# First loads in another order over the two DMA queues, with the work that follows them on VectorE, ScalarE and TensorE reordered

## The chip, the cores and the metric

The kernel runs on one core of a Trainium2 chip. A core has five engines, each with its own in-order instruction stream: TensorE (PE in the profile, its weight loads PEld), VectorE (DVE), ScalarE (ACT), GpSimd (POOL) and SyncE (SP). SP and ACT issue the transfers of this kernel; 16 DMA engines carry them out. The metric is the time of one execution on the device in microseconds (us).

## The reference

One transformer block with adaptive layer norm: 2048 tokens of width 512, 32 heads of 16, a feed-forward width of 1792, all in bf16. The part that matters here is the first layer norm with its modulation, and the projections that read its result.

```python
mod = (_silu(c) @ w_mod).reshape(c.shape[0], 6, 1, -1)
sa, ca, ga, sb, cb, gb = (mod[:, 0].copy(), ...)
h = _layernorm(x, axis=-1) * (1 + ca) + sa
x = x + ga * _A_ref(h, A_wqkv, A_wo)          # attention, softmax over 2048 keys
h = _layernorm(x, axis=-1) * (1 + cb) + sb
x = x + gb * _B_ref(h, B_w_gate, B_w_up, B_w_down)
```

`sa` is the first block of 512 columns of `silu(c) @ w_mod`, `ca` the second.

## The kernel before

The kernel has a prologue and a stream. The prologue (`prologue`, from L499) loads what the first 512 tokens need and brings them as far as q and k of the first heads; the stream then runs the attention of 32 heads, the output projection, the second norm and the feed-forward. In the stream the exponentials on ACT (`E<-ps_sc`) follow each other almost without a gap, and what else there is to do is placed between them on the other engines.

Every instruction goes through a recorder. It writes the instructions down in the order in which the Python code calls them, finds which earlier instruction on another engine each one must wait for, and emits one in-order program for each engine. The order in the prologue is written out by hand. In the stream a planner places the work by modelled times and due times; its result is an order as well, and on the chip only that order and the waits count. All instructions have the lines of the recorder's helpers in the profile: L313 matmul, L317 transpose, L326 activation, L338 `tensor_scalar`, L343 `scalar_tensor_tensor`, L330 `tensor_tensor`, L354 memset, L366 and L369 the statistics, L376 a transfer.

The prologue, in its steps:

- Loads (L505 to L517). `x0` holds tokens 0 to 255 (tiles 0 and 1 of 128 tokens each), `x1` tokens 256 to 511 (tiles 2 and 3), `x2` to `x4` the other tokens, 512 each. `wm0` is the block of `w_mod` for `sa`, `wm1` the one for `ca`; `wm2` holds the other four. `wq1`, `wq0` and `wq2` are the columns of `wqkv` for k, q and v of the first eight heads, `wr0` to `wr2` the other columns. Rows of 1 KB are moved for x0, x1, wm0 and wm1, rows of 256 bytes for wq0 to wq2.
- The conditioning vector (L538 to L540, L547). PE turns `c` (times 0.5) from a row into four columns; ACT takes the tanh of it (`tcol`); DVE makes `(tanh + 1) * c/2`, which is silu(c), the operand `sc_bf` of the products with `w_mod`.
- Statistics (`ln_stat`, two DVE instructions for a tile). Tiles 0, 2 and 3 are done on DVE; tile 1 on ACT, with an activation that sums for the mean, one that squares and sums for the variance, and one that scales (`mv<-nwx`).
- Modulation (`mod_cols`, L646). For each of eight columns of 128 values PE does four products with `sc_bf`: 16 matmuls for `sa` (columns 0 to 3, they need wm0), 16 for `ca` (columns 4 to 7, they need wm1). DVE adds the result to `modA` (zeros for `sa`, ones for `ca`).
- Warm-up (`warm_up`). Matmuls of zeros into `ps_mi` keep PE busy; nothing reads their result.
- Inverse deviation and norms. `ln_rstd` does eight small DVE steps for the four tiles together (`nwx`, `rstd`, `nwt`) and one more gives `nb`, the negative mean times the inverse deviation, which the norms on ACT use as their bias (`nwt<-mv,rstd`). Then the four norms go from `xs` to `dreg`: on DVE a `tensor_scalar`, on ACT an activation.
- Transposes, modulation of the transposed tiles (`hreg<-ps_sc,modA` and `hreg<-ps_mi,modA`, five on DVE and three on ACT, each for 128 channels by 256 tokens), and the projections to q and k. Two halves: h = 0 is tiles 0 and 1, h = 1 is tiles 2 and 3. The projections of the first half begin with channel block 3, which ACT modulates.

Of the kernel before, what the change touches and what calls it, by code (L numbers as in the profile page):

```python
# [6 lines left out]
ALU = mybir.AluOpType  # L7
# [6 lines left out]
P = 128  # L14
# [6 lines left out]
NDC = D // P  # L21
# [397 lines left out]
class _Kernel(_Recorder):  # L419
# [79 lines left out]
    def prologue(self):  # L499
        sp, act, pe, dve, pool = "sp", "act", "pe", "dve", "pool"  # L500
        xv = self.A_x.rearrange("b (t p) d -> p (b t) d", p=P)
        wmv = self.w_mod.rearrange("(a p) n -> p a n", p=P)
        wqv = self.A_wqkv.rearrange("(a p) (k n) -> p a k n", p=P, k=3)
        wq4 = self.wqkv.rearrange("p a (k n) -> p a k n", k=3)
        self.dma(sp, self.xs[:, 0:2, :], xv[:, 0:2, :], "x0")  # L505
        self.dma(act, self.crow[0:1, :], self.c, "c")
        self.dma(act, self.xs[:, 2:4, :], xv[:, 2:4, :], "x1")
        for i, q in enumerate((sp, act)):
            self.dma(q, self.wmod[:, :, D * i:D * i + D], wmv[:, :, D * i:D * i + D], "wm%d" % i)
        for k in (1, 0):  # L510
            self.dma(sp, wq4[:, :, k, 0:P], wqv[:, :, k, 0:P], "wq%d" % k)
        self.dma(sp, wq4[:, :, 2, 0:P], wqv[:, :, 2, 0:P], "wq2")
        for i in range(1, 4):
            self.dma(sp, self.xs[:, 4 * i:4 * i + 4, :], xv[:, 4 * i:4 * i + 4, :], "x%d" % (i + 1))
# [28 lines left out]
        self.act(junk, self.xs[:, 1, :], ACT.Copy, scale=1.0 / D, accum=m1)  # L543
        self.act(junk, self.xs[:, 1, :], ACT.Square, bias=m1, scale=-1.0, accum=v1[:, 0:1])
        self.act(self.mv[:, 1, 1:2], v1[:, 0:1], ACT.Copy, scale=1.0 / D)
        self.ln_stat(2)
        self.stt(self.sc_bf[:, :], self.tcol[:, :], 1.0, self.scp[:, 0, 0:NDC], ALU.add, ALU.mult)  # L547
        self.ln_stat(3)
        self.warm_up(7)
        self.mod_cols(self.scp[:, 1, 0:8], 0, range(4))  # L550
        self.warm_up(1)
        self.mod_cols(self.scp[:, 1, 0:8], 0, range(4, 8))
        self.warm_up(2)
        self.ln_rstd(0, 4)
        nb = self.nwt[:, 0:4]
        self.stt(nb, self.mv[:, 0:4, 0], -1.0, self.rstd[:, 0:4], ALU.mult, ALU.mult)
        for t in range(4):
            dst = self.tb1[:, 0, t, :]
            if t % 2 == 0:
                self.ln_norm(t, dst)  # L560
                if t == 0:
                    self.tt(dve, self.modA[:, :], self.modA[:, :], self.scp[:, 1, 0:8], ALU.add)
            else:
                self.act(dst, self.xs[:, t, :], ACT.Identity, bias=nb[:, t:t + 1], scale=self.rstd[:, t:t + 1])
# [1179 lines left out]
```

## Time and profile before

| | us |
|---|---|
| median of 3 runs | 865.73 |
| lowest and highest run | 864.06 and 866.16 |
| the profiled execution | 862.18 |
| its span | 860.4 |
| PE busy | 797.4 (93%) |
| DVE busy | 694.8 (81%) |
| ACT busy | 834.0 (97%) |
| POOL busy | 4.5 (1%) |

The span goes from the first to the last instruction of the profiled execution; 1.78 us of its time lie outside. The granted TensorE clock was 1.00. Times in the views count from the start of the span. In the timeline a row holds start, length, engine, line, operation, what is written and read, how many instructions are merged, and in brackets the idle time of the engine before them with what ended it. SPq and ACTq are the issues of transfers on SP and ACT.

The profiled execution lies under all three runs shown. Durations of single instructions come from it alone.

### The profile page before, as it was taken

The page shows a single profiled execution, that of the slowest core. Times are in us where ns is not written, and L with a number is a line of the kernel's source. Part 1 is how long each engine was busy: PE and PEld are TensorE (multiplying, and loading weights), DVE is VectorE, ACT ScalarE, POOL GpSimd, SP SyncE. Part 2 cuts the span into 40 slices and gives each one's busy share as a digit, 9 for nine tenths or more (in the row PEclk, how much of TensorE's full clock was granted, in tenths as well). Part 3 has the DMA queues.
Part 4 walks back from the last instruction along what each step waited for, and adds up shares of the span by engine and source line. Part 5 has one row for each costly group of instructions (what it writes and reads, how often), then busy time and mean ns, then how long its engine had stood idle before and what let it go on. Part 6 is the DMA issues. An engine that isn't in the chain of part 4 may idle for free.

```text
span 860.4 us, 27593 instructions
## 1 busy us (share of the span) xinstructions
PE 797.4 (93%) x12434; PEld 285.5 (33%) x12434; DVE 694.8 (81%) x1339; ACT 834.0 (97%) x748; POOL 4.5 (1%) x12
## 2 busy tenths in 40 slices
PE   7889999999999899899999999999999889998988
PEld 3333332322222222222222222222343233354456
DVE  7865989989889989988899989989987663687255
ACT  6999999999999999999999999999999999999992
POOL 1000000000000000000000000000000000000000
PEclk9999999999999999999999999999999999999999
DMA  9000000000003111210002112120134231500000
GB/s 312 9 26 17 3 9 9 10 9 9 10 4 93 44 45 33 58 33 20 10 15 82 45 32 58 34 58 11 45 92 119 80 81 43 153 11 10 21 5 14
DMA packets 63807, 38.06 MB, mean 44 GB/s; under 512 B 17389, under 2 KB 61546, under 8 KB 63690
## 3 DMA queue, kind: packets, MB, share of 16 engines
q1 hardware_dynamic: 62888, 35.52, 14.8%
q8 instruction: 97, 1.59, 0.8%
q10 hardware_dynamic: 802, 0.79, 0.3%
q14 instruction: 20, 0.16, 0.1%
HBM read 33.68 MB, written 2.61 MB: 42 GB/s over the span
## 4 chain that ended last, share of the span: by engine, by line
ACT 82%; PE 8%; DVE 5%; DMA 3%; SPq 1%; issue 1%; ACTq 0%; DVEq 0%
ACT E L326 79%; PE ps_sc L313 4%; PE ps_mi L313 3%; ACT wreg L326 3%; PE ps_pv L313 1%; DMA rb<-scr_rec 1%; DMA scr_rec<-rden 1%; SPq L376 1%; DVE st L366 1%; DVE hreg L338 1%; DMA xs<-in_A_x_dram 1%; DVE nwt L330 0%; DVE wreg L338 0%; DVE dreg L338 0%; DVE mreg L338 0%
## 5 line engine op out<-in xcount | busy, mean ns | idle before, releaser
L326 ACT ACTIVATE E<-ps_sc 128x1536 bf16<-128x1536 f32 (+2 forms) x698 | 805.5, 1343 | 11.8 <-PE ps_sc L313 11.7
L313 PE MATMUL ps_sc<-qT,kmo 32*128 32x512 bf16 (+2 forms) x1408 | 178.7, 323 | 11.3 <-ACT E L326 9.8
L313 PE MATMUL ps_sc<-qT,kme 32*128 32x512 bf16 (+2 forms) x1344 | 172.8, 331 | 13.8 <-ACT E L326 11.1
L313 PE MATMUL ps_pv<-E,vaug 128*17 128x512 bf16 (+2 forms) x2352 | 171.0, 322 | 2.3 <-DVE vaug L347 1.0
L338 DVE TENSOR_SCALAR dreg<-ps_sc 128x512 uint16<-128x512 f32 x192 | 132.3, 690 | 33.1 <-PE ps_sc L313 30.4
L338 DVE TENSOR_SCALAR mreg<-dreg 128x2048 uint16<-128x2048 uint16 x192 | 124.9, 682 | 0.4 <-PE ps_pv L313 0.4
L313 PE MATMUL ps_mi<-wreg,mreg 128*32 128x512 bf16 (+2 forms) x1504 | 110.3, 370 | 11.6 <-DVE wreg L343 6.6
L313 PE MATMUL ps_pv<-mreg,vs 128*17 128x512 bf16 (+2 forms) x1344 | 100.8, 350 | 1.4 <-DVE mreg L338 1.2
L313 PEld LDWEIGHTS ps_sc<-qT,kmo 32*128 32x128 bf16 x1408 | 48.1, 91 | 125.3 <-ACT E L326 96.4
L313 PEld LDWEIGHTS ps_sc<-qT,kme 32*128 32x128 bf16 x1344 | 45.4, 91 | 130.7 <-ACT E L326 98.9
L313 PEld LDWEIGHTS ps_pv<-E,vaug 128*17 128x17 bf16 x2352 | 52.4, 89 | 85.8 <-issue 60.3
L338 DVE TENSOR_SCALAR mreg<-ps_sc 128x512 uint16<-128x512 f32 x96 | 66.3, 691 | 17.2 <-PE ps_sc L313 15.3
L338 DVE TENSOR_SCALAR mreg<-mreg 128x2048 uint16<-128x2048 uint16 x96 | 63.0, 684 | 0.0
L313 PEld LDWEIGHTS ps_mi<-wreg,mreg 128*32 128x32 bf16 (+1 forms) x1504 | 34.0, 95 | 62.5 <-issue 20.6
L347 DVE CAST wreg<-ps_mi 128x512 bf16<-128x512 f32 x51 | 35.0, 687 | 15.4 <-PE ps_mi L313 14.6
L343 DVE SCALAR_TENSOR_TENSOR wreg<-wreg,ps_mi 128x512 bf16<-128x512 bf16 x51 | 34.9, 685 | 13.4 <-PE ps_mi L313 7.8
L313 PEld LDWEIGHTS ps_pv<-mreg,vs 128*17 128x17 bf16 x1344 | 31.2, 89 | 31.2 <-DVE mreg L338 13.8
L313 PE MATMUL ps_mi<-hreg,wreg 128*32 128x512 bf16 (+1 forms) x496 | 39.5, 377 | 2.2 <-DVE hreg L338 1.0
L313 PE MATMUL ps_mi<-wo,onorm 128*32 128x512 bf16 x480 | 37.8, 383 | 0.1
L330 DVE TENSOR_TENSOR wreg<-wreg 128x1024 bf16<-128x1024 bf16 (+1 forms) x60 | 35.7, 603 | 0.7
L330 DVE TENSOR_TENSOR onorm<-osb,rb 128x512 bf16<-128x512 f32 (+2 forms) x43 | 23.5, 548 | 12.1 <-DMA rb<-scr_rec 11.8
L313 PE MATMUL ps_mi<-mreg,hreg 128*32 128x512 bf16 x384 | 32.5, 384 | 0.0
(147 smaller groups left out, 571.0 us busy)
## 6 DMA issues: line engine op xcount, KB each, us to landing
mreg<-in_B_w_up_dram SPq DMA_DIRECT2D x25, 256.0 KB, 3.2
mreg<-in_B_w_gate_dram SPq DMA_DIRECT2D x21, 256.0 KB, 3.0
rb<-scr_rec SPq DMA_DIRECT2D x96, 32.0 KB, 1.8
mreg<-in_B_w_down_dram SPq DMA_DIRECT2D x12, 256.0 KB, 2.7
dreg<-in_B_w_down_dram SPq DMA_DIRECT2D x9, 256.0 KB, 3.7
mreg<-in_w_mod_dram SPq DMA_DIRECT2D x1, 2048.0 KB, 11.5
out_dram<-xs SPq DMA_DIRECT2D x15, 128.0 KB, 1.7
xs<-in_A_x_dram SPq DMA_DIRECT2D x3, 512.0 KB, 8.2
```

What stands on the lines that cost most here:

```text
L313: return self.rec("pe", lambda e: e.matmul(out, lhsT, rhs, start=start, stop=stop, tile_position=tp), [lhsT, rhs], [out], cost=(n, int(rhs ...
L326: return self.rec("act", lambda e: e.activation(out, in_, func, scale=scale, **kw), rd, wr, cost=self.cost("act", out, [in_], "act"))
L330: return self.rec(eng, lambda e: e.tensor_tensor(out, a, b, op), [a, b], [out], cost=self.cost(eng, out, [a, b], "tt"))
L338: return self.rec(eng, lambda e: e.tensor_scalar(out, a, s1, s2, **kw), rd, [out], cost=self.cost(eng, out, [a], "ts") + (60 if len(rd) > ...
L343: return self.rec("dve", lambda e: e.scalar_tensor_tensor(out, a, s, b, op0=op0, op1=op1), rd, [out], cost=self.cost("dve", out, [a, b], " ...
L347: return self.rec(eng, lambda e: e.tensor_copy(out, in_), [in_], [out], cost=self.cost(eng, out, [in_], "ts"))
L366: return self.rec("dve", lambda e: e.bn_stats(out, in_), [in_], [out], cost=self.cost("dve", out, [in_], "bn"))
L376: return e.dma_start(out, in_)
```

## The change

Loads: `x1` moves from ACT's queue to SP's, second behind `x0`. `wm1` moves up to second on ACT's queue behind `c`, and `wm0` comes third on SP's. `wq1` moves from SP's queue to ACT's, third there.

| queue | before | after |
|---|---|---|
| SP | x0, wm0, wq1, wq0, wq2, x2, x3, x4, wr0, wr1, wr2, wm2 | x0, x1, wm0, wq0, wq2, x2, x3, x4, wr0, wr1, wr2, wm2 |
| ACT | c, x1, wm1 | c, wm1, wq1 |

DVE: the silu operand is made ahead of tile 2's statistics, where it stood between tile 2's and tile 3's. PE: the products with `wm1` come first, then three warm-up matmuls, then the products with `wm0`; before, wm0's came first, with one warm-up matmul between. Norms: tile 3 goes from ACT to DVE, so that DVE norms tiles 0, 2 and 3. Behind that the order of instructions is the same on every engine, and so is their number.

```diff
         self.dma(sp, self.xs[:, 0:2, :], xv[:, 0:2, :], "x0")
         self.dma(act, self.crow[0:1, :], self.c, "c")
-        self.dma(act, self.xs[:, 2:4, :], xv[:, 2:4, :], "x1")
-        for i, q in enumerate((sp, act)):
+        self.dma(sp, self.xs[:, 2:4, :], xv[:, 2:4, :], "x1")
+        for i, q in ((1, act), (0, sp)):
             self.dma(q, self.wmod[:, :, D * i:D * i + D], wmv[:, :, D * i:D * i + D], "wm%d" % i)
-        for k in (1, 0):
-            self.dma(sp, wq4[:, :, k, 0:P], wqv[:, :, k, 0:P], "wq%d" % k)
+        for k, q in ((1, act), (0, sp)):
+            self.dma(q, wq4[:, :, k, 0:P], wqv[:, :, k, 0:P], "wq%d" % k)
         self.dma(sp, wq4[:, :, 2, 0:P], wqv[:, :, 2, 0:P], "wq2")
...
+        self.stt(self.sc_bf[:, :], self.tcol[:, :], 1.0, self.scp[:, 0, 0:NDC], ALU.add, ALU.mult)
         self.ln_stat(2)
-        self.stt(self.sc_bf[:, :], self.tcol[:, :], 1.0, self.scp[:, 0, 0:NDC], ALU.add, ALU.mult)
         self.ln_stat(3)
         self.warm_up(7)
+        self.mod_cols(self.scp[:, 1, 0:8], 0, range(4, 8))
+        self.warm_up(3)
         self.mod_cols(self.scp[:, 1, 0:8], 0, range(4))
-        self.warm_up(1)
-        self.mod_cols(self.scp[:, 1, 0:8], 0, range(4, 8))
         self.warm_up(2)
...
             dst = self.tb1[:, 0, t, :]
-            if t % 2 == 0:
+            if t != 1:
                 self.ln_norm(t, dst)
```

## The prediction

> **What bounds the kernel now.** I read the page first: the span, and the shares of the chain of waits that ended last.
>
> ```profile
> span 860.4 us, 27593 instructions
> ...
> ACT 82%; PE 8%; DVE 5%; DMA 3%; SPq 1%; issue 1%; ACTq 0%; DVEq 0%
> ```
>
> ScalarE (ACT) holds 82% of that chain, almost all of it exponentials of the attention. No instruction behind the prologue changes its order on any engine, so the change can only move the moment at which this stream begins. The bound that matters is therefore that of the prologue, read in the chain followed back from 16 us:
>
> ```profile
> 1.37 4.39 DMA xs<-in_A_x_dram
> ...
> 5.86 0.71 DVE st L366
> ...
> 7.69 0.18 DVE nwx L338
> ...
> 9.47 0.70 ACT dreg L326
> 10.19 0.80 ACT dreg L326
> 10.99 0.46 ACT hreg L326
> ...
> 11.50 0.28 PE ps_sc L313
> ```
>
> The columns are start, length, what. The prologue waits for x1 (tokens 256 to 511), which lands at 1.37 + 4.39 = 5.76 us. Then come the statistics of tiles 2 and 3 on VectorE (DVE), the inverse deviation from 7.69, two norms on ACT (tiles 1 and 3), the first modulation on ACT, and at 11.50 the first q projection. The timeline shows what stands beside it:
>
> ```profile
> 0.80 0.45 SPq L376 DMA_DIRECT2D xs<-in_A_x_dram  x1
> ...
> 1.30 0.46 SPq L376 DMA_DIRECT2D mreg<-in_w_mod_dram  x1
> 1.37 0.43 ACTq L376 DMA_DIRECT2D xs<-in_A_x_dram  x1
> ...
> 1.81 1.70 SPq L376 DMA_DIRECT2D wreg<-in_A_wqkv_dram  x3
> 1.83 0.54 ACTq L376 DMA_DIRECT2D mreg<-in_w_mod_dram  x1
> ...
> 2.40 1.28 ACT L326 ACT_TABLE_LOAD   x1 [2.40 <-issue]
> ...
> 3.55 5.21 SPq L376 DMA_DIRECT2D xs<-in_A_x_dram  x3
> 3.63 0.69 DVE L366 BATCH_NORM_STATS2 st<-xs 128x6 f32<-128x512 bf16 x1 [0.89 <-DMA xs<-in_A_x_dram]
> ...
> 3.69 2.11 PE L313 MATMUL ps_mi<-dreg 128*128 128x512 bf16 x7
> 3.79 0.17 ACT L326 ACTIVATE tcol<-ps_sc 128x4 f32<-128x4 f32 x1
> ...
> 5.45 0.20 ACT L326 ACTIVATE mv<-nwx 128x1 f32<-128x1 f32 x1
> ...
> 6.69 0.15 DVE L343 SCALAR_TENSOR_TENSOR sc_bf<-tcol,ps_sc 128x4 bf16<-128x4 f32 x1
> 6.75 0.69 DVE L366 BATCH_NORM_STATS2 st<-xs 128x6 f32<-128x512 bf16 x1
> ...
> 6.89 0.55 PE L313 MATMUL ps_sc<-sc_bf,mreg 128*128 128x1 bf16 x16 [1.10 <-DVE sc_bf L343]
> ...
> 9.37 0.55 PE L313 MATMUL ps_sc<-sc_bf,mreg 128*128 128x1 bf16 x16 [1.69 <-DMA mreg<-in_w_mod_dram]
> ...
> 9.79 0.59 PE L313 MATMUL ps_mi<-dreg 128*128 128x512 bf16 x2
> 9.96 0.16 DVE L330 TENSOR_TENSOR modA<-modA,ps_sc 128x8 f32<-128x8 f32 x1 [0.20 <-PE ps_sc L313]
> ...
> 10.04 0.41 DVE L338 TENSOR_SCALAR dreg<-xs,mv,rstd 128x512 bf16<-128x512 bf16 x1
> 10.22 0.72 PE L317 MATMUL ps_sc<-ident,dreg 128*128 128x128 bf16 x10
> ...
> 10.81 1.69 DVE L338 TENSOR_SCALAR hreg<-ps_sc,modA 128x256 bf16<-128x256 bf16 x5 [0.36 <-PE ps_sc L317]
> ...
> 13.98 15.93 ACT L326 ACTIVATE E<-ps_sc 128x1536 bf16<-128x1536 f32 x14 [0.22 <-PE ps_sc L313]
> ...
> 15.34 0.68 DVE L366 BATCH_NORM_STATS2 st<-xs 128x6 f32<-128x512 bf16 x1
> ```
>
> Three waits end close together ahead of the modulation at 10.81: the statistics chain, TensorE (PE) waiting at 9.37 for wm1, the second block of the modulation weights, and ACT busy with tile 3 until 10.99. All three must move for the stream to begin earlier. The change touches all three.
>
> **x1 behind x0 on SP's queue.** The DMA view shows which queue moved packets, in the first 3 us, then to 3.45, then to 5 (packets, MB, share; q1 is SP's queue, q10 is ACT's):
>
> ```profile
> q1 hardware_dynamic: 260, 0.26, 31.0%
> ...
> q1 hardware_dynamic: 160, 0.15, 106.2%
> q10 hardware_dynamic: 2, 0.00, 1.3%
> ...
> q1 hardware_dynamic: 324, 0.33, 59.6%
> q10 hardware_dynamic: 255, 0.26, 47.0%
> ```
>
> x0 is 256 rows of 1 KB, so the 260 packets by 3.0 are x0. SP's next transfer, wm0, had the engines almost alone until 3.45 (160 packets), while q10's bulk began only there, about 2.1 us after x1's issue at 1.37. x1 then took 1.55 us beside wm0 (255 packets). In the changed kernel x1 stands where wm0 stood, and wm1 stands where x1 stood. So x1 gets 160 packets by 3.45 and its other 96 at 324 / 1.55 = 209 per us: done at 3.45 + 0.46 = 3.9. Its last packets were seen about 5.0 and it landed at 5.76, so 0.76 more; x0 took from 3.0 to 3.6, where its statistics begin, so 0.6. x1 lands at 4.5 to 4.7 and its statistics begin 0.1 later (5.76 to 5.86): I take 4.7 where 5.86 was, a gain of 1.16. DVE doesn't stand in the way: with x0's statistics at 3.63 and 6.75 - 5.86 = 0.89 for a tile with the silu operand behind it, it is free at 4.52.
>
> [...]
>
> **The silu operand ahead of the second statistics.** It takes 6.75 - 6.69 = 0.06 us of DVE's issue out of the path between tiles 2 and 3, so rstd begins at 7.69 - 1.16 - 0.06 = 6.47. It brings an in-order wait: sc_bf needs the tanh, and both statistics now stand behind it, and behind them everything on DVE. The tanh ends at 3.79 + 0.17 = 3.96. ACT's third issue is now wq1 in place of wm1 and its second is wm1 in place of x1: 0.54 for 0.43, and the 1.70 / 3 = 0.57 of a wq issue for 0.54, so the table load moves by about 0.14 to 2.54 and ends at 3.82: the tanh moves by hardly 0.05. Cost nothing, covered by the 0.5 us until DVE is free at 4.52. If ACT's third issue stalled as SP's three x loads do (5.21 / 3 = 1.74 each), the tanh would end near 5.2, the statistics begin near 5.4, and tile 1's statistics on ACT, now done at 5.45 + 0.20 = 5.65, near 6.9: a gain of some 0.7 instead, still no loss.
>
> **Norms.** With rstd at 6.47, tile 1's norm on ACT starts at 9.47 - 1.22 = 8.25, ends at 9.05, and ACT, without tile 3 (0.80), is free from there. DVE gets tile 3 for 0.41 (as tile 2's row). It stands after modA and tile 2, and the first modulation stands behind it. Ready times on DVE, were modA not late: tile 2 at 10.04 - 1.22 = 8.82, tile 3 from 9.23 to 9.64, modulation at about 9.65 in place of 10.81. Before, DVE idled 0.36 there for the transposes, which pays most of the 0.41.
>
> **wm1 first, three warm-up matmuls between.** Now PE does wm1's sixteen products, three matmuls, then wm0's sixteen. Landing times before:
>
> ```profile
> xs<-in_A_x_dram SPq DMA_DIRECT2D x3, 512.0 KB, 8.2
> ...
> mreg<-in_w_mod_dram SPq DMA_DIRECT2D x1, 512.0 KB, 4.6
> mreg<-in_w_mod_dram ACTq DMA_DIRECT2D x1, 512.0 KB, 7.5
> wreg<-in_A_wqkv_dram SPq DMA_DIRECT2D x3, 128.0 KB, 7.4
> ```
>
> wm0 landed at 1.30 + 4.6 = 5.9, wm1 at 1.83 + 7.5 = 9.33. In the change wm1 begins at 3.45, at q10's 255 / 1.55 = 165 packets per us: 512 packets end at 6.55 and land at about 7.25. wm0 begins at 3.9 at 209 per us, ends at 6.35 and lands at about 7.05. PE is through its seven matmuls at 5.80. The first products start at 7.25, the warm-ups 0.42 later (9.37 to 9.79), three of them take 3 x 0.215 = 0.64 (9.79 to 10.22 for two), so the second products start at 8.31 in place of 9.37: a gain of 1.06. modA follows 0.59 behind (9.96 - 9.37) at 8.90, tile 2 at 8.98, tile 3 at 9.39, the modulation at 9.80 on DVE; by the transposes, 10.81 - 9.37 = 1.44 behind, 9.75. So PE's branch ends last by some 0.1 us, and the two extra warm-ups (0.43) are nearly bare. ACT's modulation at 9.8 is 1.2 ahead of 10.99.
>
> The projections need wq1 and wq0 at 11.50 - 1.05 = 10.45. They are behind 1.5 MB as before and landed about 7.4 after issue (three issues from 1.81, 0.57 apart), so the last by 10.35; now wq1 isn't behind anything but wm1. x2 lands at 3.55 + 8.2 = 11.75 and is wanted at 15.34 - 1.05 = 14.29. Nothing charged for either.
>
> **The sum.** The start of the exponentials moves by 1.05 us, 13.98 to 12.93, and all later work with it. The profiled execution took 862.18 us, of which the span is 860.4: 861.1. The three runs shown (864.06 to 866.16, median 865.73) lie above that execution; against their median it is 865.73 - 1.05 = 864.7. Bounds of the gain: upward 1.3, if wm1 lands by 7.0 and the statistics begin at 4.52; downward through wm1, below.
>
> **The rivals.**
>
> *Turn-taking (chance 0.17).* x1 shares from the start with wm1. x0, x1 and an equal piece of wm1 are 768 packets; of the rows above 262 had moved by 3.0, 424 by 3.45 and 1003 by 5.0, so 768 by 4.37. x1 lands near 5.05, the gain is 0.7: 861.5, or 865.0 by the median. For it speaks the even share after 3.45, against it the 2 packets of q10 before that.
>
> *wm1 late, slower (0.10).* PE takes its work in order; wm1 now stands ahead of three warm-ups and wm0's products. If wm1 lands as late as before, at 9.33, the second products start at 9.37 + 1.06 = 10.43 and the modulation at 11.87: 1.06 later than now, 863.2 and 866.8. It decides from a landing of 9.37 - 1.06 = 8.31 on. Against it: x1 no longer stands ahead of wm1 on q10, and x0, x1, wm0 and wm1 together are 1536 packets, 1003 of which had moved by 5.0; at the 579 / 1.55 = 374 per us of that row the rest is through at 6.4, even with wm1 last.
>
> *The order of the data doesn't follow the order of issue (0.08).* x1 lands at 5.76 again and the time stays at 862.2 (865.7). The rows of q1, where each load follows the last, speak against it.
>
> *More than the prologue's wait (0.08).* The stream of exponentials may also catch a wait behind 13.98 that the earlier start lets it miss, for instance on the statistics of tile 4 at 15.34; a second gain of the same size or somewhat more makes 2.1 to 2.9 in all, about 859.6 (863.2). Nothing in the order of instructions asks for it.
>
> **How the numbers follow.** The forecast, a gain of 0.9 to 1.3, has the remaining 0.57, and its time is 864.7. About 0.3% (2.6 us) is what a measurement of this kernel can tell from no change; every case but the last lies inside that, but the runs themselves spread by 2.1 us and the profiled execution lies 3.5 under their median. So faster 0.11 (the last case and the spread), same 0.83, slower 0.06 (the late wm1 and the spread). The range runs from 862.7 (through most of the last case) to 866.4 (most of the way to the late wm1).
>
> **What would show it.** In the changed profile: tile 2's statistics on DVE near 4.7 (5.15 by turn-taking, 5.86 if nothing moved); the first products on PE near 7.25, waiting for w_mod; the second near 8.3; modA near 8.9; the first modulations at 9.8 on both engines; the exponentials from 12.9. Wrong would be wm1 after 8.3, a table load that starts after 2.6, a projection waiting for wqkv, or a start of the exponentials that moved by 1 us with an end that did not.

## The result, and the profile after

Over 20 executions of each kernel the median went from 864.93 us to 862.56 us. The ratio of the new time to the old is 0.9969, 95% interval [0.9961, 0.9977]: faster by 0.31%, 2.7 us by the ratio and 2.4 us by the medians. The forecast was a gain of 1.05 us and 864.7 us with a range down to 862.7, so the time lies just under the range and the gain is well over twice the sum.

The profiled execution of the changed kernel tells the opposite at first sight. It took 864.73 us, the longest of its 20. From the page:

```profile
span 862.6 us, 27597 instructions
...
ACT 77%; PE 14%; DVE 6%; DMA 2%; issue 1%; SPq 0%; DVEq 0%
```

The span is 2.2 us longer than the 860.4 of before, and PE's share of the chain went from 8% to 14%. The timeline of the same execution, the rows that answer to those of before:

```profile
4.76 0.69 DVE L366 BATCH_NORM_STATS2 st<-xs 128x6 f32<-128x512 bf16 x1 [0.20 <-DMA xs<-in_A_x_dram]
...
7.85 0.56 PE L313 MATMUL ps_sc<-sc_bf,mreg 128*128 128x1 bf16 x16 [2.02 <-DVE nwt L330]
...
8.27 1.44 PE L313 MATMUL ps_mi<-dreg 128*128 128x512 bf16 x3
...
9.50 0.61 PE L313 MATMUL ps_sc<-sc_bf,mreg 128*128 128x1 bf16 x16
...
10.15 0.16 DVE L330 TENSOR_TENSOR modA<-modA,ps_sc 128x8 f32<-128x8 f32 x1 [1.58 <-PE ps_sc L313]
...
11.71 1.69 DVE L338 TENSOR_SCALAR hreg<-ps_sc,modA 128x256 bf16<-128x256 bf16 x5 [0.75 <-PE ps_sc L317]
...
14.87 2.37 ACT L326 ACTIVATE E<-ps_sc 128x1536 bf16<-128x1536 f32 x2 [0.22 <-PE ps_sc L313]
```

Tile 2's statistics begin at 4.76 as forecast (4.7). Then PE stands idle for 2.02 us until the first products. The view names a DVE step as what ended that wait, but the DVE operand had been ready since 4.6; what came last was wm1, whose landing lies 6.3 us behind its issue at 1.38. What follows is new: three warm-up matmuls take 1.44 us, and in the profile of before two took 0.59. The stages by windows (start:end, length, busy time of PE, PEld, DVE, ACT and POOL with counts, then granted TensorE clock, DMA share, GB/s), first in the prologue, then far behind it:

```profile
8.10:11.50 3.40, 3.40 (x40) 2.02 (x37) 1.28 (x5) 0.81 (x1) 0.00 (x0) 0.50 1.13 320
...
178.80:185.40 6.60, 6.60 (x47) 1.08 (x39) 3.41 (x7) 5.29 (x6) 0.00 (x0) 0.50 0.04 11
```

TensorE was granted half its clock from 8.06 for 3.41 us, and again from 178.7 for 6.83 us. The late wm1 and the stretch in the prologue together moved the start of the exponentials to 14.87; the later stretch cost another 1.8 us or so (the exponentials are 0.44 us behind those of before ahead of it and 2.2 to 2.3 behind them after it). The profile of before, with a clock of 1.00 in the same window, has neither:

```profile
8.10:11.50 3.40, 2.07 (x35) 1.50 (x35) 2.63 (x13) 1.99 (x4) 0.00 (x0) 1.00 1.11 329
```

So two single executions were set against each other that differ by more than the change. The experiments therefore list the mean granted clock of every execution. A stretch of 3.41 us at half clock takes 0.5 x 3.41 / 862 = 0.002 off that mean: 1.000 is none, 0.998 one, 0.996 two.

### The profile page after: what moved, and what is told of

It reads as the page before. It is cut to its first block, busy times and chain, and to the rows that moved or that the text cites. A ratio compares the mean times of both kernels' runs of the same rounds, so it can differ in the third digit from the quotient of the medians.

```text
span 862.6 us, 27597 instructions
## 1 busy us (share of the span) xinstructions
PE 801.2 (93%) x12436; PEld 286.5 (33%) x12436; DVE 694.8 (81%) x1340; ACT 833.8 (97%) x747; POOL 4.5 (1%) x12
## 4 chain that ended last, share of the span: by engine, by line
ACT 77%; PE 14%; DVE 6%; DMA 2%; issue 1%; SPq 0%; DVEq 0%
ACT E L326 74%; PE ps_sc L313 6%; PE ps_mi L313 5%; PE ps_pv L313 3%; ACT wreg L326 3%; DVE mreg L338 1%; DVE st L366 1%; DVE hreg L338 1%; DMA rb<-scr_rec 1%; DMA den<-scr_den 0%; DMA xs<-in_A_x_dram 0%; SPq L376 0%; DVE nwt L330 0%; DVE wreg L338 0%; DVE dreg L338 0%
## 5 line engine op out<-in xcount | busy, mean ns | idle before, releaser
L313 PE MATMUL ps_sc<-qT,kmo 32*128 32x512 bf16 (+2 forms) x1408 | 178.7, 323 | 11.3 <-ACT E L326 9.8
```

The costliest lines, as they stand in the source:

```text
L313: return self.rec("pe", lambda e: e.matmul(out, lhsT, rhs, start=start, stop=stop, tile_position=tp), [lhsT, rhs], [out], cost=(n, int(rhs ...
```

## The experiments

Theory 1 says that the gain beyond the sum comes from half-clock stretches of TensorE that the kernel before has more of. Theory 2 says that the loads of the kernel before usually land later than in the one profile, with nothing in the clock. The runs come in three groups, each on one chip, with the kernel before run beside it; a ratio is always against the kernel before of the same group. The first group held the two kernels and the two halves of the change.

*The kernel before once more.* No edit.

> The kernel before once more, to see how its executions spread and which granted clock each had. Theory 1 (clock): the measured gain of 2.4 to 2.7 us is the 1.05 us of the sum and, on top, half-clock stretches of TensorE of 3.41 us in the prologue, each about 1.8 us dear, which the kernel before has in more of its executions than the changed one (there 9 of 20 have a mean clock under 0.9995). Expected: ratio 1.000, more than 9 of its executions under 0.9995, and these 1 us or more above the others. Theory 2 (pure shift): the loads of the kernel before usually land later than in the one execution that I read; the clocks are as in the changed kernel, and the executions with clock 1.000 still lie 2.3 us or more above those of the changed kernel (862.3).

Ratio 1.000 [0.9987, 1.0013]. All 12 executions had a clock of 0.998 or less, and so had the 35 others of this kernel in the group. The two later groups add 64 more with the same outcome: of 111 listed executions of this kernel none is above 0.998. The execution that the prediction read, with 1.000, was the exception. Among the 35, those at 0.998 average 863.86 us and those at 0.996 865.15, so a further stretch goes with 1.3 us; the later groups give 1.2 and 1.1. From the timeline and windows of this profile:

```profile
10.32 0.58 PE L313 MATMUL ps_sc<-sc_bf,mreg 128*128 128x1 bf16 x16 [2.45 <-DMA mreg<-in_w_mod_dram]
...
10.76 1.01 PE L313 MATMUL ps_mi<-dreg 128*128 128x512 bf16 x2
...
12.56 1.68 DVE L338 TENSOR_SCALAR hreg<-ps_sc,modA 128x256 bf16<-128x256 bf16 x5 [1.14 <-PE ps_sc L317]
...
16.57 1.45 ACT L326 ACTIVATE E<-ps_sc 128x1536 bf16<-128x1536 f32 x1 [0.21 <-PE ps_sc L313]
```

```profile
8.10:11.50 3.40, 1.18 (x18) 0.71 (x19) 2.09 (x11) 1.52 (x2) 0.00 (x0) 0.50 1.11 329
11.50:14.90 3.40, 3.40 (x25) 2.82 (x24) 1.68 (x5) 1.59 (x3) 0.00 (x0) 0.50 1.10 338
```

The clock was halved from 8.11 to 14.94, two stretches in a row. The exponentials begin at 16.57, 2.59 us later than in the profile before: 0.95 of it because wm1's products start at 10.32 for 9.37, and the other 1.64 behind that, at half clock.

*The changed kernel once more.* No edit.

> The changed kernel once more. Both theories: ratio 0.996 to 0.998. Theory 1: in an execution without a half-clock stretch the exponentials start 1 us before 13.98, near 12.9, or 13.2 with the first products at 7.85; with one in the prologue at 14.9 as in the profile at hand. Theory 2: they start at 14.9 in nearly every execution, and before later still.

Ratio 0.997 [0.9958, 0.9982]; 9 of 12 executions at 0.999 or 1.000. Its profiled execution had no half-clock stretch in the prologue:

```profile
4.93 0.69 DVE L366 BATCH_NORM_STATS2 st<-xs 128x6 f32<-128x512 bf16 x1 [0.21 <-DMA xs<-in_A_x_dram]
...
6.17 0.54 PE L313 MATMUL ps_sc<-sc_bf,mreg 128*128 128x1 bf16 x16
...
6.57 0.81 PE L313 MATMUL ps_mi<-dreg 128*128 128x512 bf16 x3
...
7.96 0.55 PE L313 MATMUL ps_sc<-sc_bf,mreg 128*128 128x1 bf16 x16 [0.58 <-DMA mreg<-in_w_mod_dram]
...
8.66 0.15 DVE L330 TENSOR_TENSOR modA<-modA,ps_sc 128x8 f32<-128x8 f32 x1
...
9.71 1.68 DVE L338 TENSOR_SCALAR hreg<-ps_sc,modA 128x256 bf16<-128x256 bf16 x5 [0.24 <-PE ps_sc L317]
...
9.76 0.56 ACT L326 ACTIVATE hreg<-ps_sc,modA 128x256 bf16<-128x256 bf16 x1 [0.49 <-PE ps_sc L317]
...
12.87 4.62 ACT L326 ACTIVATE E<-ps_sc 128x1536 bf16<-128x1536 f32 x4 [0.22 <-PE ps_sc L313]
```

This is the prologue of the forecast: modulation at 9.71 (9.80 was written down), exponentials from 12.87 (12.93). PE is never idle longer than 0.58 us between 3.5 us and the transposes. The lead did not last to the end: the exponentials are 1.2 us ahead of those of before up to 500 us, and a stretch of 6.83 us at half clock from 810.8 costs 2.1, so that this execution ends later than the one of before.

*The loads alone.*

```diff
 # loads as in the changed kernel; the rest as before
-        self.dma(act, self.xs[:, 2:4, :], xv[:, 2:4, :], "x1")
+        self.dma(sp, self.xs[:, 2:4, :], xv[:, 2:4, :], "x1")
...
```

> Only the new order of the loads over the two queues; the order on VectorE, ScalarE and TensorE is that of before. Both theories: x1's statistics begin near 4.8, both blocks of the modulation weights have landed by 8, so the second products start near 8.3 and ScalarE is free of tile 3's norm at 9.8: a gain of about 0.9 us (ratio 0.9990). Theory 1 adds that the gap on TensorE ahead of the products stays below 2.1 us and the one between them goes: fewer half-clock stretches, ratio 0.997 to 0.998. Theory 2: ratio about 0.997 with no change in the clocks.

Ratio 0.9994 [0.9982, 1.0006]; all 12 executions at 0.998 or less. Statistics earlier, as expected, but:

```profile
8.19 0.54 PE L313 MATMUL ps_sc<-sc_bf,mreg 128*128 128x1 bf16 x16 [1.86 <-DMA mreg<-in_w_mod_dram]
...
14.59 3.71 ACT L326 ACTIVATE E<-ps_sc 128x1536 bf16<-128x1536 f32 x3 [0.22 <-PE ps_sc L313]
```

```profile
9.10:12.40 3.30, 3.30 (x32) 2.49 (x30) 1.86 (x7) 1.87 (x4) 0.00 (x0) 0.50 1.10 347
```

The old order of products waits for wm0, which the new loads put last of the four. PE idles 1.86 us and the clock halves at 9.08; in this profile that takes more than the loads bring (exponentials at 14.59, for 13.98 before). Theory 1's ratio (0.997 to 0.998) was missed although both gaps came out as it had asked: 1.86 us is below 2.1, and the gap between the two groups of products is gone. What failed is its premise that a gap of this length keeps the clock. The interval holds the 0.9990 of the sum as well as no gain, so a gain of 0.9 us by the loads is neither shown nor excluded.

*The rest alone.*

```diff
 # operand, products, warm-ups and norm as in the changed kernel; loads as before
-        self.dma(sp, self.xs[:, 2:4, :], xv[:, 2:4, :], "x1")
+        self.dma(act, self.xs[:, 2:4, :], xv[:, 2:4, :], "x1")
...
```

> The loads as before; the silu operand ahead, the products of the second block first with three warm-up matmuls behind, tile 3's norm on VectorE. The products now wait for wm1, near 9.3, and wm0's come 1.06 behind: by the sum the modulation comes 1.06 us later than before, ratio 1.0012. Theory 1: TensorE then stands from 5.8 to 9.3 with nothing to do, 3.5 us, so nearly every execution has a half-clock stretch in the prologue and loses 1.8 us more: ratio 1.003. Theory 2: ratio 1.001.

Ratio 1.0005 [0.999, 1.002]; all 12 at 0.998 or less. This is theory 2's number, and the interval excludes the 1.003 of theory 1. That number was set wrongly: it charged a stretch in the prologue against a kernel before without one, and the first group shows that the kernel before has one as a rule, so the two cancel. The wait was also shorter than expected, with wm1's products from 8.69 in place of 9.3 and 1.83 us of idle time in place of 3.5:

```profile
8.69 0.54 PE L313 MATMUL ps_sc<-sc_bf,mreg 128*128 128x1 bf16 x16 [1.83 <-DVE nwt L330]
```

Here too the profile has 3.41 us at half clock, from 10.69. This kernel doesn't tell the theories apart. What the two halves show is that neither makes the whole gain alone and both together do.

The second group, in which the kernel before had a median of 866.88 us, changed the clock without the loads, and the parts that the sum had priced.

*The kernel before with its gaps filled.*

```diff
-        self.warm_up(7)
+        self.warm_up(12)
         self.mod_cols(self.scp[:, 1, 0:8], 0, range(4))
-        self.warm_up(1)
+        self.warm_up(9)
```

> The kernel before with more warm-up matmuls in TensorE's two gaps: twelve for seven, nine for one. Nothing else moves; no load or operand comes earlier. Theory 1 (clock): all 47 executions of the kernel before whose clock is listed so far had a mean clock under 0.9985, at least one half-clock stretch of 3.41 us. With TensorE busy in the 3.41 us behind the first rise of the clock that stretch goes: most executions at 0.999 to 1.000, exponentials from 14.0 to 14.9 (as wm1 lands), ratio 0.998 to 0.9987. Theory 2 (the loads alone make the gain): the clock may rise, but the time stays, ratio 0.9995 to 1.0005.

Ratio 0.9976 [0.9964, 0.9988]. Of 12 executions 8 are at 0.999 or 1.000, and none of the 35 of the kernel before in this group. Thirteen matmuls whose result nothing reads, and not one load or operand earlier, give 2.0 us, more than theory 1 had expected (0.998 to 0.9987):

```profile
3.69 4.04 PE L313 MATMUL ps_mi<-dreg 128*128 128x512 bf16 x12
...
7.97 2.10 PE L313 MATMUL ps_mi<-dreg 128*128 128x512 bf16 x9
...
9.91 0.54 PE L313 MATMUL ps_sc<-sc_bf,mreg 128*128 128x1 bf16 x16
...
14.49 3.71 ACT L326 ACTIVATE E<-ps_sc 128x1536 bf16<-128x1536 f32 x3 [0.21 <-PE ps_sc L313]
```

```profile
8.10:11.50 3.40, 3.40 (x41) 2.09 (x39) 2.43 (x13) 1.63 (x3) 0.00 (x0) 1.00 1.13 321
```

Theory 2 falls here as the whole explanation: it expected 0.9995 or more. The four executions at 0.998 or less don't show where their stretches lay.

*One warm-up matmul between the two groups, for three.*

```diff
         self.mod_cols(self.scp[:, 1, 0:8], 0, range(4, 8))
-        self.warm_up(3)
+        self.warm_up(1)
```

> The changed kernel with one warm-up matmul between the two groups of products, as before, in place of three. By the prediction's sum these two are 0.43 us, nearly bare: ratio 0.9965, faster than the changed kernel. By the execution with the exponentials from 12.86, TensorE waits 0.58 us for wm0 behind them, so they cost nothing, and theory 1 has them keep the clock up: more executions under 0.9985 than 10 of 32, ratio 0.9973 to 0.998.

Ratio 0.999 [0.9975, 1.0004], and 11 of 12 executions at 0.998 or less, more stretches and a smaller gain than theory 1 expected (0.9973 to 0.998). Two matmuls fewer, and by the middle values two thirds of the gain go; the interval just touches that of the changed kernel (up to 0.9977):

```profile
6.93 0.38 PE L313 MATMUL ps_mi<-dreg 128*128 128x512 bf16 x1
...
8.44 0.55 PE L313 MATMUL ps_sc<-sc_bf,mreg 128*128 128x1 bf16 x16 [1.13 <-DMA mreg<-in_w_mod_dram]
...
14.34 3.71 ACT L326 ACTIVATE E<-ps_sc 128x1536 bf16<-128x1536 f32 x3 [0.21 <-PE ps_sc L313]
```

```profile
9.60:12.90 3.30, 3.30 (x24) 2.62 (x23) 2.06 (x7) 1.94 (x4) 0.00 (x0) 0.50 1.11 350
```

The second products start at 8.44 with one warm-up matmul ahead of them as with three (7.96 above): they wait for wm0. The two others cost nothing. That they help to keep the clock rests on the count, 11 of 12 here against 10 of 32 of the changed kernel in the result and the first group; the third group, below, has 8 of 12 for the changed kernel itself, so the size of what they carry isn't settled.

*Tile 3's norm back on ACT.*

```diff
-            if t != 1:
+            if t % 2 == 0:
```

> The changed kernel with tile 3's norm back on ScalarE. Both theories: ScalarE does tile 1 and tile 3 to about 10.0, and its first modulation starts there in place of 9.76: 0.2 to 0.3 us of the gain, ratio 0.9973; the clocks as in the changed kernel (about a third of the executions under 0.9985). If the norm's move carried more, the ratio would be 0.998 or above.

Ratio 0.9976 [0.996, 0.9993], 8 of 12 executions at 0.998 or less, where about a third was expected. Its profile has a full clock in the prologue and exponentials from 13.19, 0.2 to 0.3 later than 12.87 and 13.02 of the changed kernel, as expected. The ratio can't tell such a step.

*The changed kernel with eleven warm-up matmuls for seven.*

```diff
-        self.warm_up(7)
+        self.warm_up(11)
```

> The changed kernel with eleven warm-up matmuls for seven ahead of the first products. Theory 1: the prologue's half-clock stretch, which the changed kernel still has in some executions, goes in all; 0.2 to 0.4 us less on the mean, ratio 0.9962 to 0.997, against which up to 0.5 us stands where wm1 lands before the warm-ups end (6.7 to 7.3). Theory 2: no gain, ratio 0.997 to 0.9978.

Ratio 0.9963 [0.995, 0.9976], 7 of 12 executions at 1.000. In the profile the prologue ran at full clock, with exponentials from 13.06; two stretches, of 6.83 and 3.41 us, fell later, from 177.1 and 812.0. The third group, with a kernel before of 866.28 us, set this kernel against the changed one on one chip, with two more.

> The changed kernel beside the three that follow, on the same chip. Theory 1 (clock): ratio 0.997, a quarter to a third of the executions under 0.9985, all of the kernel before's under it. Rival (earlier loads make the gain, clock a by-product): the same.

> The changed kernel with eleven warm-up matmuls for seven once more, to compare with the changed kernel on one chip. Theory 1: 0.2 to 0.4 us under the changed kernel's mean, ratio 0.996 to 0.997. Rival: equal or slower, ratio 0.997 to 0.998.

The changed kernel: 0.9981 [0.9966, 0.9996], 8 of 12 executions at 0.998 or less, more than the expected third, and more than in the result and the first group together (10 of 32). Eleven warm-ups: 0.9973 [0.9961, 0.9984], 9 of 12 at 0.998 or less, in the rival's range and not in theory 1's. The intervals lie over each other, so no gain of the filled kernel over the changed one is shown. In both profiles the prologue ran at full clock and a stretch fell later, from 810.4 and from 667.3.

*Nine and five warm-up matmuls for seven and three.*

```diff
-        self.warm_up(7)
+        self.warm_up(9)
         self.mod_cols(self.scp[:, 1, 0:8], 0, range(4, 8))
-        self.warm_up(3)
+        self.warm_up(5)
```

> The changed kernel with nine warm-up matmuls for seven ahead of the first products and five for three between the two groups. Theory 1: the 3.41 us behind the first rise are busy wherever the rise falls, nearly no half-clock stretch in the prologue; the second products start at 8.4 to 8.6 for 7.96 to 8.44, up to 0.4 us later. Ratio 0.9962 to 0.997. Rival: only the later products show, ratio 0.9973 to 0.998.

Ratio 0.9965 [0.995, 0.9981]; 7 of 10 at 0.998 or less, with a full clock in the prologue of the profile and 6.83 us at half clock from 176.8. Faster than the kernel before, not told apart from the changed one.

*The loads alone, with thirteen warm-up matmuls for seven.*

```diff
 # loads as in the changed kernel, order of the products as before
-        self.warm_up(7)
+        self.warm_up(13)
```

> Only the new order of the loads, and thirteen warm-up matmuls for seven; the order of the products, the silu operand and tile 3's norm as before. With the loads alone the ratio was 0.9994 and all 12 executions were under 0.9985. Theory 1: the warm-ups fill the gap ahead of the products, at least 8 of 12 executions at 0.9985 or more, ratio 0.9968 to 0.9978, as the changed kernel within 0.4 us although the products stand in the old order. Rival (the order of the products is what makes the loads count): ratio 0.999 or above.

Ratio 0.9964 [0.9951, 0.9978], slightly better than theory 1's range; of 8 executions 4 are at 1.000, fewer than the two thirds it expected. With the loads alone, in the first group, the ratio was 0.9994 [0.9982, 1.0006] and no execution was above 0.998; the intervals lie apart. So the rival falls: the order of the products isn't needed for the gain, and six more matmuls of zeros ahead of them are enough:

```profile
8.49 0.54 PE L313 MATMUL ps_sc<-sc_bf,mreg 128*128 128x1 bf16 x16 [1.52 <-DVE nwt L330]
...
13.69 3.71 ACT L326 ACTIVATE E<-ps_sc 128x1536 bf16<-128x1536 f32 x3 [0.22 <-PE ps_sc L313]
```

## Why the prediction was wrong

**What held.** The chain through the statistics, the modulation and the start of the exponentials: tile 2's statistics at 4.76 to 5.09 for the forecast 4.7, and in the two profiles with a full clock in the prologue modulation at 9.71 and 9.86 for 9.80, exponentials at 12.87 and 13.02 for 12.93. Against 13.98 that is 1.0 to 1.1 us, the 1.05 of the sum. All later work moved with it as far as the next stretch at half clock: exponentials at 340 us are 1.19 earlier in the second profile of the changed kernel than in the profile before. That the start of the exponentials came out so close is in part luck, as the landings below show. What the prediction had named as a sign of being wrong, a start that moved by 1 us with an end that did not, showed in that profile too: its end is 1.5 us later, for the stretch from 810.8.

**The step that failed** is the one in "The sum" that carries 1.05 us from the profiled execution to the median of the runs ("against their median it is 865.73 - 1.05 = 864.7"). It took the difference of 3.5 us between the two for spread. At least in part it was something that this execution alone lacked: each of 111 others, with a mean clock of 0.998 or less, had at least one stretch of TensorE at half clock. A reduction of such stretches could not appear in a sum made from an execution without any, and so the sum put it at nothing. The size: the mean clock went from 0.9967 (35 executions) to 0.9990 (12) in the first group, (0.0033 - 0.0010) x 862 / 0.5 = 4.0 us less at half clock, 1.16 stretches at 1.2 us each, 1.4 us. With the 1.05 that makes 2.45; the means of that group differ by 864.65 - 862.15 = 2.50. The rest of the distance from 864.7 to 862.56 is the kernel before itself, whose median of 20 was 864.93 where three runs had given 865.73.

The split into 1.05 and 1.4 is an estimate. The same sum for the changed kernel in the third group gives 0.6 + 1.05 = 1.6 for a measured 1.56, but for the one with eleven warm-ups there 1.6 for 2.64. At the same mean clock of 0.998 the third group has 863.79 us (5 executions of the changed kernel) against 865.20 (7 of the kernel before), 1.4 us apart. The single execution of before at 1.000 took 862.18 us and the eleven of the changed kernel at 1.000 in the result took 862.29 on average; a comparison at full clock on one chip is missing.

**The two extra warm-up matmuls** were booked as 0.43 us "nearly bare". They were not: they were hidden behind wm0, and the ratio was 0.999 with one warm-up between the groups and 0.9969 to 0.9981 with three, though on different chips and with intervals that touch.

**The landings of the modulation weights** were off, in ways that cancelled by luck. wm1 was put at 7.25 by the 165 packets per us that ACT's queue had moved in the profile before. In the second profile of the changed kernel the packets from 3.45 to 5 were

```profile
q10 hardware_dynamic: 399, 0.41, 76.5%
q1 hardware_dynamic: 136, 0.12, 31.9%
```

that is 257 per us for ACT's queue and 88 for SP's, no even share. wm1 was there when PE got to it at 6.17, for 7.25, and wm0 landed at 7.9 for the 7.05 of the sum: the first products came 1.1 us early, the wait behind them took 0.7 of it back, and the second products began at 7.96 for 8.31. In the first profile the same window gave 359 and 118 packets and wm1 still landed only near 7.7, 6.3 us behind its issue for 4.7 in the second, so the landing itself varies by more than a microsecond between executions.

**The rivals.** Turn-taking, with tile 2's statistics at 5.15, isn't excluded by that time: they begin at 4.76, 4.93 and 5.09 in the three profiles of the changed kernel, and at 4.82 to 5.20 in the seven others with the same loads. Either way it is 0.4 us. The equal piece of wm1 in its sum no run shows: by 3.45 ACT's queue had moved 7 packets in the first profile of the changed kernel and 2 in the second, for 426 and 408 of SP's, and from 3.45 to 5 about three times as many as SP's. A late wm1 didn't occur: 7.7 is under the 8.31 from which it decides. The rival with more than the prologue's wait gave the right size (2.1 to 2.9 us) for a wrong reason, a wait in the stream.

## What to carry to other kernels

Where the profiled execution lies outside the spread of the runs, find out what it has or lacks before a sum made on it is set against their median; the mean clock of every execution told it here. In a prologue with TensorE waits of 1 to 2 us, count how busy TensorE is in the 3.41 us after its clock rises, as below: filler matmuls in such gaps alone gave 0.9976, where the whole reordering gave 0.9969 to 0.9981. A reordering of loads can be hidden by the clock: here the loads alone gave nothing that could be measured (0.9994), and with six filler matmuls more they gave 0.9964.

## What the runs showed of the hardware

In five of the 14 profiled executions the half clock began 3.41 us behind the first rise of the clock (8.06 behind 4.64, 8.11 behind 4.70, 9.08 behind 5.67, 9.54 behind 6.13, 10.69 behind 7.28; the times are in the trace's record of the granted clock), with TensorE busy for 0.19 to 0.35 of the time between. In each of the 14 I took these 3.41 us and counted the share of them in which columns were streamed, a 512-column matmul as 0.215 us from its start, its spacing at full clock (four starts 0.215 to 0.217 us apart from 4.80 in the first profile of the changed kernel):

| execution | rise, us | share | clock after |
|---|---|---|---|
| loads alone | 5.67 | 0.19 | half |
| changed, first | 4.64 | 0.28 | half |
| one warm-up | 6.13 | 0.32 | half |
| before, second | 4.70 | 0.33 | half |
| rest alone | 7.28 | 0.35 | half |
| before, first | 4.58 | 0.36 | full |
| tile 3 on ACT | 5.50 | 0.39 | full |
| changed, third | 4.86 | 0.44 | full |
| changed, second | 5.30 | 0.48 | full |
| the five filled ones | 4.34 to 6.46 | 0.66 to 0.87 | full |

In the prologue, where nearly all columns are streamed through the whole array (weighted as below, the profile before and the first of the changed kernel have the same 0.36 and 0.28), the two kinds separate: by this count the highest share that lost the clock is 0.35 and the lowest that kept it 0.36. It isn't as sharp as that: one matmul of 512 columns is 0.06 of the window, and if each is placed at the end of its record instead of its start, the two are 0.39 and 0.41. The windows that were up to about a third busy lost the clock. The rise itself falls anywhere between 4.3 and 7.3 us with the same matmuls at the start of the prologue, so which gap lies inside the window changes from one execution to the next, and one kernel has executions of both kinds: the kernel before kept the clock with 0.36 and lost it with 0.33, the changed one kept it with 0.44 and 0.48 and lost it with 0.28. This is a reading over 14 executions; no run varied the share by itself.

In the stream, where most matmuls use a part of the array (11932 of the 12436 in the first profile of the changed kernel), stretches at half clock came too, in seven of the 14 profiles and always near 177 to 179, 667 or 810 to 815 us. The plain share doesn't separate them there: the windows just ahead of them have 0.99 to 1.46, since matmuls on parts of the array overlap there (four of 128 x 17 start within 0.01 us at 175.50 in the same profile and take 0.39 us together). Weighted by the part of the array that each matmul uses (its rows times its columns over 128 x 128), those eight windows have 0.23 to 0.31. Of the 3413 such windows at full clock between 15 and 850 us in the 14 profiles, 23 are at 0.31 or below, and all eight stretches follow one of these 23; none follows any of the 3390 above. So a low share of work on the array goes with the loss of the clock in the stream as well; why 15 of the 23 kept it stays open.

That matters for the count of executions. In the five kernels with filled gaps the profiles show a full clock in the prologue, and still 29 of their 54 executions have a mean clock of 0.998 or less. So such a mean says that there was a stretch, not that it lay in the prologue, and the 18 of 44 of the changed kernel may lie in the stream as well. Why its count was higher in the third group than in the first stays open.
